# Key sums on TensorE for the first twelve head pairs, weight rounding on ScalarE, and an order that knows the shared port

## The chip, the cores and the metric

The kernel runs on one core of one Trainium2 chip. The metric is the device time of one execution in microseconds (us); of the kernel before there are three timed runs, 1079.8, 1080.3 and 1081.45 us, with a median of 1080.3 us. Five engines work side by side: PE (TensorE, whose weight loads are a row of their own, PEld), DVE (VectorE), ACT (ScalarE), POOL (GpSimd) and SP, which here only issues DMAs.

## The reference

An attention with random features feeds a gated two-layer network.

```python
# attention: batch 8, 8 heads, 576 rows, head dimension 64, 128 features
phi(x) = exp(x @ omega.T - |x|^2/2 - max over features) / sqrt(128)   # x scaled by 64**-0.25
q_p, k_p = phi(q), phi(k)
kv  = sum over rows s of k_p[s, m] * v[s, d]
z   = sum over rows s of k_p[s, m]
num = q_p @ kv
den = (q_p @ z) + 1e-6
x   = num / den                      # 4608 tokens x 512
# network: 512 -> 2048 -> 512
h = x @ w_in
out = (h * sigmoid(h)) @ w_out
```

The weights `w_in` and `w_out` arrive as 64-bit floats, everything else in 32 bits.

## The kernel before, in words

**Attention.** The 64 heads are worked in 32 pairs, called windows in the code and pairs here, numbered 0 to 31. The 2 x 576 rows of a pair lie as nine chunks of 128 rows; the fifth chunk holds the last 64 rows of the first head and the first 64 of the second. For keys (k) and queries (q) alike: PE projects eight chunks into two PSUM banks (`project`, L304) and the mixed chunk into a third (`project_mid`, L311); ACT squares the rows and DVE sums the squares (L292, L296); DVE takes the maxima (L318, L320), makes the shift from them (`shift`, L324 and L325), and ACT takes the exponential, for pairs 0 to 7 straight from PSUM (L340), from pair 8 on in one piece over all nine chunks after DVE has lowered them into SBUF (L345, L348, L354).

Then comes the part that the change touches. POOL adds up the key exponentials of each head over its chunks (`sums`, L360, L362, L365: 1,152 columns become 2 x 128). PE multiplies the 256 sums by a matrix of ones, so that every partition holds both key sums (`zsum`, L369). ACT copies them from PSUM to SBUF in three blocks, for the first head, the mixed chunk and the second head (`zcopy`, L377, L378). DVE multiplies each of the nine query chunks with its block and accumulates along the row (`denom`, L405, with an accumulator read behind each), and takes the reciprocals (L410). POOL scales the query exponentials with them, three chunks at a time (`normal`, L415). PE transposes the nine chunks (`turn`, L421), ACT copies them out (L425), and PE multiplies them by the pair's key-value matrix (`numer`, L438; `kv`, L385, makes that matrix). ACT and DVE split the product into a high and a low part, the network's input x (L457, L461).

**Weights.** 32 blocks of 128 x 512 are turned from 64-bit to 32-bit floats by one ACT instruction (L488) and three DVE instructions each (`word`, L500, L502, L506), and then split: POOL rounds the high part (`weight_high`, L516) and subtracts it for the low one (`weight_low`, L520). Later POOL makes eight sets of sums of `w_out` blocks (L536 to L539) and splits those as well (L543, L547).

**Network.** Each product is three passes of 128 x 512 on PE (L567: high by high, high by low, low by high). The first tile of 512 tokens uses the weights as they come; the later tiles are worked in pairs with seven products in place of eight, read their split weights back from DRAM, and need ACT (L600, L609) and DVE (L605, L613) for activations, differences and low parts.

**Order.** Nothing orders itself at run time: each engine works its queue in order. The queues come from a list scheduler in the file (`Plan`). Each unit of work has an engine, a planned duration, a key (when it is wanted), the units it needs, and the ring buffers and PSUM banks it takes and frees; `run` repeatedly takes the unit that can start first. The pool of banks `att` has two banks. Pools `acc` (four) and `h` (two) are open to attention only before the network needs them, and `acc` again between the first tile's end and the first paired tile.

## Time and profile before

| | |
|---|---|
| timed runs, median | 1080.3 us |
| profiled execution | 1083.05 us |
| its span | 1081.3 us |
| instructions | 16865 |
| granted PE clock, mean | 0.968 |

| engine | busy us | share of the span |
|---|---|---|
| PE | 1010.0 | 93% |
| DVE | 755.3 | 70% |
| ACT | 633.2 | 59% |
| POOL | 323.7 | 30% |

The span is what the profile covers; the time of the same execution is 1.75 us longer. Shares over the whole span hide that the program has stages: PE is busy 5 to 7 tenths of the first 81 us, nearly all of the time from about 330 us on, and in between by turns. So the profile is read by stretches.

### The profile page before, as it was taken

The page shows a single profiled execution, that of the slowest core. Times are in us where ns is not written, and L with a number is a line of the kernel's source. Part 1 is how long each engine was busy: PE and PEld are TensorE (multiplying, and loading weights), DVE is VectorE, ACT ScalarE, POOL GpSimd, SP SyncE. Part 2 cuts the span into 40 slices and gives each one's busy share as a digit, 9 for nine tenths or more (in the row PEclk, how much of TensorE's full clock was granted, in tenths as well). Part 3 has the DMA queues.
Part 4 walks back from the last instruction along what each step waited for, and adds up shares of the span by engine and source line. Part 5 has one row for each costly group of instructions (what it writes and reads, how often), then busy time and mean ns, then how long its engine had stood idle before and what let it go on. Part 6 is the DMA issues. An engine that isn't in the chain of part 4 may idle for free.

```text
span 1081.3 us, 16865 instructions
## 1 busy us (share of the span) xinstructions
PE 1010.0 (93%) x5708; PEld 797.7 (74%) x5708; DVE 755.3 (70%) x1761; ACT 633.2 (59%) x1155; POOL 323.7 (30%) x390
## 2 busy tenths in 40 slices
PE   5667999898879999999999999999999999999998
PEld 4445767576657877777777777777777788888886
DVE  6897797978855789866677888667667642323565
ACT  4667768566546666666666667666666433333343
POOL 2665465586872122222122221222222100000000
PEclk7687999999989999999999999999999999999999
DMA  8686686788767666767766567666644586665454
GB/s 292 222 264 211 205 270 236 253 297 283 245 209 258 200 197 194 233 201 223 236 219 199 181 211 247 200 221 230 195 147 140 178 293 212 213 200 189 160 183 149
DMA packets 96325, 235.01 MB, mean 217 GB/s; under 512 B 17264, under 2 KB 33776, under 8 KB 96240
## 3 DMA queue, kind: packets, MB, share of 16 engines
q1 hardware_dynamic: 96096, 233.87, 65.8%
q8 instruction: 46, 0.75, 0.3%
q14 instruction: 39, 0.32, 0.1%
q10 hardware_dynamic: 144, 0.07, 0.0%
HBM read 197.20 MB, written 36.70 MB: 216 GB/s over the span
## 4 chain that ended last, share of the span: by engine, by line
PE 73%; DVE 18%; ACT 4%; issue 3%; POOL 1%; DMA 1%; SPq 0%; DVEq 0%; ACTq 0%; POOLq 0%
PE ps_h L567 30%; PE ps_acc L567 28%; DVE prod L405 5%; PE ps_att L304 4%; PE ps_att L385 3%; PE ps_att L421 2%; PE ps_att L438 2%; DVE g L502 1%; DVE mxk L320 1%; DVE mxq L320 1%; DVE g L500 1%; PE ps_att L311 1%; DVE g L506 1%; DVE nbk L324 1%; PE ps_att L369 1%
## 5 line engine op out<-in xcount | busy, mean ns | idle before, releaser
L567 PE MATMUL ps_h<-x,w 128*128 128x512 f32 x1728 | 452.0, 404 | 0.6 <-POOL w L520 0.6
L567 PE MATMUL ps_acc<-ts,wo 128*128 128x512 f32 x1536 | 384.0, 395 | 0.2 <-DVE nbq L324 0.2
L567 PEld LDWEIGHTS ps_h<-x,w 128*128 128x128 f32 x1728 | 319.0, 191 | 71.1 <-POOL w L520 1.5
L567 PEld LDWEIGHTS ps_acc<-ts,wo 128*128 128x128 f32 x1536 | 284.4, 188 | 60.1 <-POOL wo L520 0.7
L613 DVE TENSOR_TENSOR ts<-g,ts 128x512 fp32r<-128x512 f32 x224 | 159.2, 723 | 128.4 <-ACT ts L609 127.7
L609 ACT CAST ts<-g 128x512 fp32r<-128x512 f32 x224 | 138.7, 622 | 116.0 <-PE ps_acc L567 81.6
L415 POOL TENSOR_TENSOR hq<-hq,rd 128x384 f32<-128x384 f32 x96 | 90.5, 967 | 309.7 <-DVE rd L410 290.8
L600 ACT ACTIVATE g<-ps_h 128x512 f32<-128x512 f32 x128 | 76.6, 598 | 148.5 <-PE ps_h L567 147.1
L405 DVE CUSTOM_DVE_ANT_0 prod<-hq,zb 128x128 f32<-128x128 f32 x288 | 97.3, 338 | 50.7 <-ACT zb L378 31.3
L605 DVE TENSOR_TENSOR g<-g,g 128x1024 f32<-128x1024 f32 x64 | 79.8, 1255 | 32.2 <-ACT g L600 32.2
L360 POOL TENSOR_TENSOR t<-hk 128x256 f32<-128x256 f32 x64 | 49.2, 789 | 151.6 <-ACT hk L354 132.2
L354 ACT ACT_TABLE_LOAD x46 | 59.0, 1283 | 28.4 <-DVE hk L345 14.2
L600 ACT ACT_TABLE_LOAD x44 | 56.5, 1283 | 0.8
L292 ACT ACTIVATE nat<-nat 128x576 f32<-128x576 f32 x64 | 43.5, 686 | 15.6 <-DMA nat<-qn 9.4
L320 DVE TENSOR_REDUCE mxq<-ps_att 128x4 f32<-128x512 f32 x53 | 34.2, 684 | 24.0 <-PE ps_att L304 24.0
L425 ACT COPY en<-ps_att 128x384 f32<-128x384 f32 x76 | 34.8, 478 | 22.4 <-PE ps_att L421 21.8
L385 PE MATMUL ps_att<-hk,v 128*64 128x128 f32 x580 | 41.4, 293 | 4.1 <-issue 2.3
L304 PE MATMUL ps_att<-oms,rawq 64*128 64x128 f32 x424 | 36.7, 294 | 8.8 <-ACT zb L378 5.7
L304 PEld LDWEIGHTS ps_att<-oms,rawq 64*128 64x128 f32 x424 | 30.4, 195 | 19.0 <-ACT zb L378 6.9
L385 PEld LDWEIGHTS ps_att<-hk,v 128*64 128x64 f32 x580 | 34.0, 146 | 14.1 <-issue 10.6
L421 PE MATMUL ps_att<-ident,hq 128*128 128x128 f32 x228 | 36.7, 283 | 8.1 <-DVE hk L348 3.9
L421 PEld LDWEIGHTS ps_att<-ident,hq 128*128 128x128 f32 x228 | 27.6, 144 | 17.1 <-issue 6.7
(139 smaller groups left out, 1185.5 us busy)
## 6 DMA issues: line engine op xcount, KB each, us to landing
w<-w_d SPq DMA_DIRECT2D x128, 512.0 KB, 3.7
wo<-w_d SPq DMA_DIRECT2D x112, 512.0 KB, 4.4
rawk<-kT SPq DMA_DIRECT2D x32, 352.0 KB, 4.4
rawq<-qT SPq DMA_DIRECT2D x32, 352.0 KB, 4.3
...
```

The lines of the kernel that those rows point to most:

```text
L304: nc.tensor.matmul(ps[:, i * M : (i + 1) * M], raw[r, o : o + P], oms[r], start=True, stop=True)
L320: nc.vector.tensor_reduce(m[:, 5 * j : 5 * j + 4], ps.rearrange("p (c m) -> p c m", m=M), AX.X, ALU.max)
L354: nc.scalar.activation(h, h, AF.Exp)
L385: nc.tensor.matmul(ps[j * D : (j + 1) * D, :M], vt[:, c + j], e[:, c], start=i == 0, stop=i == 4)
L405: nc.vector.tensor_tensor_reduce(out=prod, in0=e[:, c], in1=zb[:, j], scale=1.0, scalar=GUARD, op0=ALU.mult, op1=ALU.add, accum_out=den[:, ...
L415: nc.gpsimd.tensor_tensor(e[:, c], e[:, c], rd[:, c].unsqueeze(2).broadcast_to([P, 3, M]), ALU.mult)
L421: nc.tensor.transpose(ps[:, i * P : (i + 1) * P], T["h", n, "q"][:, 3 * g + i], ident)
L567: nc.tensor.matmul(ps, w(a), x[:, b], start=first and n == 0, stop=last and n == 2, **more)
L600: nc.scalar.activation(T["g", p, q, u][:, f % 2], T["ph", t, f], AF.Silu)
L605: nc.vector.tensor_tensor(out, a, b, ALU.subtract)
L609: nc.scalar.copy(g[:, 0], T["g", p, SOURCE[j], i // 2][:, i % 2])
L613: nc.vector.tensor_tensor(g[:, 1], T["g", p, SOURCE[j], i // 2][:, i % 2], g[:, 0].bitcast(F32), ALU.subtract)
```

## The change

- `FEW = 12`. For pairs 0 to 11, `sums`, `zsum` and `zcopy` are gone. `zsum_all` takes their place: twenty matmuls of 128 columns on PE, whose moving operand is the key exponentials themselves and whose stationary operand is ones, or, for the mixed chunk, `half`, ones in one head's partitions and zeros in the other's. They leave the three blocks side by side in one PSUM bank. Five go into all 128 partitions for each head; for the mixed block five go into partitions 0 to 63 and then five into 64 to 127.
- For those pairs `denom` reads the blocks from PSUM, and the bank is free only after the ninth chunk. The scaling is one DVE instruction over 1,152 columns (`normal_all`) in place of three on POOL. Pairs 12 to 31 are as before.
- The rounding of the high parts, 32 blocks and 16 of the sums, goes from POOL to ACT (`nc.scalar.copy`).
- The scheduler gets a time `port` that the marked units share: POOL's, and those of DVE with two SBUF operands, may not overlap in its plan. Most planned durations and DMA times are lowered, by about an eighth; `den` goes from 2.3 to 3.1 and `wlo` from 1.05 to 1.3.

```diff
+FEW = 12
@@ Plan
-    def add(self, name, eng, dur, key, fn, after=(), order=(), alloc=(), free=(), banks=0, table=None, lat=0.0):
+    def add(self, name, eng, dur, key, fn, after=(), order=(), alloc=(), free=(), banks=0, table=None, lat=0.0, port=False):
...
-                    t = max(t, free_at[e])
+                    t = max(t, free_at[e], port if u["port"] else 0.0)
...
+            if u["port"]:
+                port = t + dur
@@ attention_mlp
+    half = const.tile([P, 2, P], F32, tag="half", name="half")
+    nc.vector.memset(half, 0.0)
+    for j in range(2):
+        nc.vector.memset(half[j * D : (j + 1) * D, j], 1.0)
...
+    def zsum_all(n, ps):
+        e = T["h", n, "k"]
+        for b, (j, cols, rows) in enumerate(((0, P, 0), (0, D, 0), (1, D, D), (1, P, 0))):
+            at = (0, 1, 1, 2)[b] * M
+            for i in range(5):
+                nc.tensor.matmul(
+                    ps[rows : rows + cols, at : at + M], half[:, j, :cols] if i == 4 else ones[:, :cols],
+                    e[:, MID if i == 4 else 5 * j + i], start=i == 0, stop=i == 4,
+                )
+        T["zb", n] = ps[:, : 3 * M].rearrange("p (j m) -> p j m", m=M)
+
+    def normal_all(n):
+        e, rd = T["h", n, "q"], T["rd", n]
+        nc.vector.tensor_tensor(e, e, rd.unsqueeze(2).broadcast_to([P, NC, M]), ALU.mult)
...
-        nc.gpsimd.tensor_copy(parts_of(i)[0], T["w", i])
+        nc.scalar.copy(parts_of(i)[0], T["w", i])
...
-        nc.gpsimd.tensor_copy(o[:, 0], T["whole", i][:, b])
+        nc.scalar.copy(o[:, 0], T["whole", i][:, b])
@@ the units of a pair
+        few = n < FEW
+        if few:
+            add(zn, "PE", 1.8, at(n, 6, 26), lambda ps, n=n: zsum_all(n, ps), after=e["k"] + e["q"], banks=1, free=[("h", n, "k")],
+                order=[("z", n - 1)] if n else [])
+        else:
+            add(("sums", n), "POOL", 3.2, at(n, 6, 25), lambda n=n: sums(n), after=e["k"], port=True,
...
-        add(("den", n), "DVE", 2.3, at(n, 8, 34.2), lambda n=n: denom(n), after=e["q"] + [("zc", n)],
-            order=[("den", n - 1)] if n else [], alloc=[("den", ("den", n)), ("rd", ("rd", n))], free=[("zb", n)])
+        add(("den", n), "DVE", 3.1, at(n, 8, 34.2), lambda n=n: denom(n), after=e["q"] + [zn if few else ("zc", n)],
+            order=[("den", n - 1)] if n else [], alloc=[("den", ("den", n)), ("rd", ("rd", n))],
+            free=[bk(zn) if few else ("zb", n)], port=not few)
+        if few:
+            add(("norm", n, 0), "DVE", 1.25, at(n, 9, 37), lambda n=n: normal_all(n), after=[("den", n)],
+                free=[("rd", n)], port=True)
@@ the weights
-        add(("wh",) + i, "POOL", 0.9, key - 1, lambda: weight_high(i), after=[("wd",) + i + (2,)], alloc=list(more))
-        add(("wlo",) + i, "POOL", 1.05, key, lambda: weight_low(i), after=[("wh",) + i])
+        add(("wh",) + i, "ACT", 0.55, key - 1, lambda: weight_high(i), after=[("wd",) + i + (2,)], alloc=list(more))
+        add(("wlo",) + i, "POOL", 1.3, key, lambda: weight_low(i), after=[("wh",) + i], port=True)
```

The order moves with it. Line numbers are those of each file: L304, L311, L369, L385, L393, L405, L461, L500, L502, L506, L520 and L567 of the kernel before are L311, L318, L390, L407, L415, L427, L483, L522, L524, L528, L542 and L589 of the changed one.

PE from the products of pair 4 (`en,kw`) to the projection of pair 6 (`oms,rawk`), before:

```order
L438 MATMUL ps_att<-en,kw 64x64 x2
L567 MATMUL ps_h<-x_918,w_978 128x512 x3
L567 MATMUL ps_acc<-ts,wo 128x512 x9
L369 MATMUL ps_att<-es,ones 128x256
L567 MATMUL ps_acc<-ts,wo 128x512 x3
L393 MATMUL ps_att<-ident,kt 128x128
L567 MATMUL ps_h<-x_386,w_1123 128x512 x3
L567 MATMUL ps_h<-x_575,w_1123 128x512 x3
L567 MATMUL ps_h<-x_753,w_1123 128x512 x3
L304 MATMUL ps_att<-oms,rawk 128x128 x8
```

The same place in the changed kernel, from the last fifteen of the twenty matmuls on:

```order
L379 MATMUL ps_att<-hk,ones 64x128 x4
L379 MATMUL ps_att<-hk,half 64x128
L379 MATMUL ps_att<-hk,ones 64x128 x4
L379 MATMUL ps_att<-hk,half 64x128
L379 MATMUL ps_att<-hk,ones 128x128 x4
L379 MATMUL ps_att<-hk,half 128x128
L589 MATMUL ps_acc<-ts,wo 128x512 x12
L415 MATMUL ps_att<-ident,kt 128x128
L589 MATMUL ps_h<-x_372,w_1186 128x512 x3
L589 MATMUL ps_h<-x_573,w_1186 128x512 x3
L311 MATMUL ps_att<-oms,rawk 128x128 x8
```

One matmul of 256 columns became twenty of 128, and between them and the next projection, which takes both banks of `att`, stand 18 network matmuls where 12 stood.

DVE ahead of the denominators of pair 4, which begin four rows behind this piece (one more of those rows is a weight block's L506); L500, L502 and L506 are the three instructions of a weight block. Before:

```order
L506 SCALAR_TENSOR_TENSOR g_748<-g_584,g_748 128x512
L500 TENSOR_SCALAR g_849<-g_742 128x512
L500 TENSOR_SCALAR g_890<-g_745 128x512
L502 SCALAR_TENSOR_TENSOR g_890<-g_890 128x512
L506 SCALAR_TENSOR_TENSOR g_890<-g_745,g_890 128x512
L318 TENSOR_REDUCE mxq<-ps_h 128x1
L461 TENSOR_TENSOR x_918<-ps_att,x_918 128x512
L461 TENSOR_TENSOR xr<-ps_att,xr 128x64
L324 TENSOR_TENSOR nbq<-mxq,sqq 128x1
L325 SCALAR_TENSOR_TENSOR nbq<-nbq,sqq 128x1
L502 SCALAR_TENSOR_TENSOR g_849<-g_848,g_849 128x512
```

And in the changed kernel, down to the first row of those denominators:

```order
L528 SCALAR_TENSOR_TENSOR g_489<-g_400,g_489 128x512
L303 TENSOR_REDUCE sqk<-nat 128x9
L522 TENSOR_SCALAR g_489<-g_617 128x512
L522 TENSOR_SCALAR g_715<-g_622 128x512
L524 SCALAR_TENSOR_TENSOR g_715<-g_715 128x512
L528 SCALAR_TENSOR_TENSOR g_715<-g_622,g_715 128x512
L303 TENSOR_REDUCE sqq<-nat 128x9
L483 TENSOR_TENSOR x_956<-ps_acc,x_956 128x512
L483 TENSOR_TENSOR xr<-ps_acc,xr 128x64
L427 ISA prod,den<-hq,ps_acc 128x128
```

Counted from the program's start, DVE has finished 11 weight blocks at this point before and 8 now; the denominators read `ps_acc`, a PSUM bank, in place of `zb`.

POOL's first work, before:

```order
L360 TENSOR_TENSOR t<-hk 128x256 x2
L362 TENSOR_TENSOR es<-t 128x256
L365 TENSOR_TENSOR es<-es,hk 64x128 x2
L415 TENSOR_TENSOR hq<-hq,rd 128x384 x3
L516 CAST w_309<-g_253 128x512
L520 TENSOR_TENSOR w_309<-g_253,w_309 128x512
```

And in the changed kernel, where up to the sums of `w_out` blocks only low parts are left on it:

```order
L542 TENSOR_TENSOR w_436<-g_250,w_436 128x512
L542 TENSOR_TENSOR w_442<-g_277,w_442 128x512
L542 TENSOR_TENSOR wo<-g_274,wo 128x512
L542 TENSOR_TENSOR w_627<-g_483,w_627 128x512
L542 TENSOR_TENSOR wo<-g_274,wo 128x512
```

More of the change, by code (lines that the diff above doesn't have):

```diff
@@ L692, in attention_mlp @@
             for j in range(3):
-                add(("top", n, who, j), "DVE", 0.3 if j == 2 else 0.7,
+                add(("top", n, who, j), "DVE", 0.26 if j == 2 else 0.62,
                     at(n, 3 * i + 1 + 0.1 * j, o + 1.2 + (4.5 if j == 2 else 0.1 * j)),
@@ L707, in attention_mlp @@
                 if n < DIRECT:
-                    add(("exp", n, who, j), "ACT", 0.4 if j == 2 else 1.15,
+                    add(("exp", n, who, j), "ACT", 0.35 if j == 2 else 1.05,
                         at(n, 3 * i + 2 + 0.1 * j, o + 1.6 + (4.4 if j == 2 else 0.1 * j)),
@@ L711, in attention_mlp @@
                 else:
-                    add(("low", n, who, j), "DVE", 0.36 if j == 2 else 0.7,
+                    add(("low", n, who, j), "DVE", 0.3 if j == 2 else 0.62,
                         at(n, 0, o + 1.5 + (4.4 if j == 2 else 0.1 * j)),
@@ L715, in attention_mlp @@
             if n >= DIRECT:
-                add(("expall",) + w, "ACT", 1.2, at(n, 0, 24 + 0.1 * i), lambda n=n, who=who: expo_all(n, who),
+                add(("expall",) + w, "ACT", 1.1, at(n, 0, 24 + 0.1 * i), lambda n=n, who=who: expo_all(n, who),
                     after=[("low", n, who, j) for j in range(3)], table="exp")
@@ L723, in attention_mlp @@
             plan.freed_by[("nb", n, who)] = [("exp" if n < DIRECT else "low", n, who, j) for j in range(3)]
[L724 to L725 removed]
         zn = ("z", n)
[L727 to L729 removed]
+        few = n < FEW
[4 more added lines that the diff above has]
+            add(("sums", n), "POOL", 3.2, at(n, 6, 25), lambda n=n: sums(n), after=e["k"], port=True,
+                order=[("sums", n - 1)] if n > FEW else [],
+                alloc=[("t", ("t", n)), ("es", ("es", n))], free=[("h", n, "k"), ("t", n)])
+            add(zn, "PE", 0.45, at(n, 7, 32), lambda ps, n=n: zsum(n, ps), after=[("sums", n)], banks=1, free=[("es", n)])
+            add(("zc", n), "ACT", 1.1, at(n, 7.1, 33.2), lambda n=n: zcopy(n), after=[zn],
+                order=[("zc", n - 1)] if n > FEW else [], alloc=[("zb", ("zb", n))], free=[bk(zn)])
         merged = n > LEAD
@@ L798, in attention_mlp @@
         last = ("out", f)
-        add(("keep2", f), "SP", 0.8, key + 4, lambda f=f: keep_second(f), after=[("wlo", "out", f)], lat=2.1,
+        add(("keep2", f), "SP", 0.8, key + 4, lambda f=f: keep_second(f), after=[("wlo", "out", f)], lat=1.75,
             free=[("wo", 0, f)])
@@ L837, in first @@
         if t == 0:
-            add(("silu", 0, f), "ACT", 1.22, key, lambda: silu(f), after=[done], alloc=[("ts", ("ts", 0, f))], table="silu")
-            add(("gl", f), "DVE", 0.7, key + 1.3, lambda: g_low(f), after=[("silu", 0, f)], free=[("ph", 0, f)])
+            add(("silu", 0, f), "ACT", 1.1, key, lambda: silu(f), after=[done], alloc=[("ts", ("ts", 0, f))], table="silu")
+            add(("gl", f), "DVE", 0.62, key + 1.3, lambda: g_low(f), after=[("silu", 0, f)], free=[("ph", 0, f)])
             return
@@ L846, in first @@
             guard = [[("wd", "out", FIRST[-1], 2)], [("co", NH - 1, 1)]][t - 1]
-        add(("silu", t, f), "ACT", 0.62, key, lambda: silu_kept(t, f), after=[done], table="silu", order=guard,
+        add(("silu", t, f), "ACT", 0.55, key, lambda: silu_kept(t, f), after=[done], table="silu", order=guard,
             alloc=[] if f % 2 else [(f"g{QUARTERS[p % 2][q]}", ("g", p, q, f % NH // 2))], free=[("ph", t, f)])
@@ L886, in differences @@
         for d in range(4):
-            add(("dif", p, d, u), "DVE", 1.2, key[d], lambda d=d: subtract(p, d, u), after=needs[d],
+            add(("dif", p, d, u), "DVE", 1.2, key[d], lambda d=d: subtract(p, d, u), port=True, after=needs[d],
                 free={2: [("g", p, 3, u)], 3: [("g", p, 0, u)]}.get(d, []))
@@ L899, in times @@
             add(("w2", p, j, u), "SP", 0.42, mm_time(pos - 14 * AHEAD_W2), lambda: get_second(p, j, u), after=w,
-                order=seconds[-1:] or [("wh", "out", FIRST[-1])], alloc=[("wo", ("w2", p, j, u))], lat=2.1)
+                order=seconds[-1:] or [("wh", "out", FIRST[-1])], alloc=[("wo", ("w2", p, j, u))], lat=1.75)
             seconds.append(("w2", p, j, u))
@@ L903, in times @@
         src = [("g", p, SOURCE[j], u)] if j in (P6, P3, P7, P4) else []
-        add(("hi", p, j, i), "ACT", 0.62, key - 4, lambda: part_high(p, j, i), after=ready(p, j, i), order=highs[-1:],
+        add(("hi", p, j, i), "ACT", 0.54, key - 4, lambda: part_high(p, j, i), after=ready(p, j, i), order=highs[-1:],
             alloc=[("ts", ("ts", p, j, i))], free=src)
-        add(("lo", p, j, i), "DVE", 0.69, key - 3, lambda: part_low(p, j, i), after=[("hi", p, j, i)], order=lows[-1:],
+        add(("lo", p, j, i), "DVE", 0.66, key - 3, lambda: part_low(p, j, i), port=True, after=[("hi", p, j, i)], order=lows[-1:],
             free=src)
@@ L955, in times @@
             add(("store", p, what), "SP", 0.42, key + 2, lambda: c_store(p, what, PAIRS[p][t], d),
-                after=[(unit, p, m) for m in range(2)], lat=2.1, free=[("c", p, what)])
+                after=[(unit, p, m) for m in range(2)], lat=1.75, free=[("c", p, what)])
     for x, f in enumerate(FIRST):
```

72 lines of the change are left out of this document (34 added, 38 removed).

## The prediction

> **What bounds the kernel now.** I read the windows view first, cut where the network's stream starts (101 us), where PE first loses its density (190 us), where the attention falls behind the network no more (328 us), and where attention ends. Its columns are busy us with instruction counts for PE, PEld, DVE, ACT and POOL, then the granted PE clock.
>
> ```profile
> 0.00:101.00 101.00, 63.74 (x437) 47.30 (x438) 83.62 (x217) 62.33 (x183) 53.51 (x69) 0.75 0.74 251
> 101.00:190.00 89.00, 84.22 (x471) 65.39 (x469) 71.76 (x158) 66.52 (x138) 49.01 (x52) 1.00 0.70 232
> 190.00:328.00 138.00, 115.19 (x714) 87.28 (x716) 107.00 (x259) 80.25 (x135) 98.07 (x121) 0.94 0.76 259
> 328.00:856.00 528.00, 526.02 (x3120) 416.12 (x3116) 390.79 (x990) 343.53 (x568) 123.08 (x149) 1.00 0.64 205
> ```
>
> Four stages with different limits. Stage A (0 to 101): DVE is busy 83.6 of 101 us, PE 63.7 at a clock of 0.75; DVE leads. Stage B (101 to 190): PE is busy 84.2 of 89; PE bounds, and 4.8 us are left. Stage C (190 to 328): PE 115.2 of 138, so 22.8 us are left; DVE 107 and POOL 98 are both high. Stage D: PE 526 of 528, nothing to gain there, and since pairs 12 to 31 keep their work, nothing much to lose.
>
> Then the chain of waits (start, length, what), of which these pieces show who leads in A and in C:
>
> ```profile
> 22.80 2.81 POOL hq L415 x3
> 30.94 2.00 POOL t L360 x2
> 98.45 6.99 PE ps_h L567 x24
> 105.44 2.72 PE ps_acc L567 x12
> 305.67 1.33 DVE prod L405
> ```
>
> In A, POOL's key sums and scaling stand on the chain. In C it is DVE's denominators, and one chunk takes 1.33 us there. The network's matmuls take 2.72 / 12 = 0.227 us each once they flow; the first 24 of them took 6.99 in place of 5.44. The timeline adds PE's own waits in A, at the transposes of pairs 2 to 4:
>
> ```profile
> 61.87 1.69 PE L421 MATMUL ps_acc<-ident,hq 128*128 128x128 f32 x6 [3.31 <-POOL hq L415]
> 77.66 0.55 PE L421 MATMUL ps_acc<-ident,hq 128*128 128x128 f32 x3 [1.63 <-POOL hq L415]
> 95.97 2.48 PE L421 MATMUL ps_acc<-ident,hq 128*128 128x128 f32 x9 [3.03 <-POOL hq L415]
> ```
>
> **Part 1, key sums on PE.** The price of a full-width 128-column matmul in 32 bits is read from two starts in stage D, and that of a half-width one, whose neighbours run in the other half of the array, from the key-value product:
>
> ```profile
> 344.68 0.38 PE L311 MATMUL ps_att<-oms,rawk 128*128 128x128 f32 x2
> 344.89 0.49 PE L421 MATMUL ps_att<-ident,hq 128*128 128x128 f32 x3
> 327.27 1.31 PE L385 MATMUL ps_att<-hk,v 128*64 128x128 f32 x20
> 328.41 1.14 PE L438 MATMUL ps_att<-en,kw 128*64 128x512 f32 x8
> 85.94 2.40 PE L385 MATMUL ps_att<-hk,v 128*64 128x128 f32 x20 [2.34 <-issue]
> ```
>
> One matmul (two records) takes 344.89 - 344.68 = 0.21 us. The ten of L385, alternating between the halves, take 328.41 - 327.27 = 1.14, or 0.114 each. The new five-and-five half-width ones don't alternate, so I price all twenty at 0.213: 4.27 us. The old matmul has 256 columns: 0.43. Net +3.84 us per pair; the lower bound, half of them at 0.114, is 10 x 0.213 + 10 x 0.114 - 0.43 = 2.84. At half clock (L385 takes 2.40 there, twice as long) it is 8.5.
>
> Where it lies: pairs 5, 6 and 7 fall in B, 3 x 3.84 = 11.5 us against 4.8 idle. I let half of that idle take it up: **B +9** (bounds +4, the cheap price with all the idle used, and +12). Pairs 8 to 11 fall in C, 15.4 us against 22.8 idle: no cost there while another engine leads. What hides it is DVE; without that cover it costs the 15.4. In A the old way to the denominators was POOL's sums, the matmul and ACT's copies:
>
> ```profile
> L360 POOL TENSOR_TENSOR t<-hk 128x256 f32<-128x256 f32 x12 | 9.4, 800 | 12.3 <-ACT hk L340 12.3
> L362 POOL TENSOR_TENSOR es<-t 128x256 f32<-128x256 f32 x6 | 5.1, 848 | 0.5
> L365 POOL TENSOR_TENSOR es<-es,hk 64x128 f32<-64x128 f32 x10 | 6.4, 644 | 0.7
> L415 POOL TENSOR_TENSOR hq<-hq,rd 128x384 f32<-128x384 f32 x15 | 12.4, 854 | 19.8 <-DVE rd L410 19.8
> L378 ACT COPY zb<-ps_acc 128x128 f32<-128x128 f32 x6 | 1.6, 264 | 0.1
> ```
>
> 2 x 0.80 + 0.85 + 2 x 0.64 = 3.7 on POOL, 0.43 / 0.75 = 0.6 on PE, 4 x 0.264 = 1.1 on ACT: 5.4 us. The new one is 4.27 / 0.75 = 5.7. I take nothing for it (bounds -1 and +3 a pair, full and half clock).
>
> [...]
>
> **Part 2, POOL emptied, DVE relieved.** DVE instructions with two SBUF operands are stretched where POOL works. First their rows in A, then in C, then D's row and whole-run minima, medians and maxima as the undisturbed price:
>
> ```profile
> L405 DVE CUSTOM_DVE_ANT_0 prod<-hq,zb 128x128 f32<-128x128 f32 x45 | 15.9, 353 | 4.0 <-ACT zb L378 1.5
> L506 DVE SCALAR_TENSOR_TENSOR g<-g,g 128x512 uint32<-128x512 uint32 x11 | 9.5, 860 | 0.2
> L500 DVE TENSOR_SCALAR g<-g 128x512 uint32<-128x512 uint32 x12 | 7.3, 621 | 0.0
> L502 DVE SCALAR_TENSOR_TENSOR g<-g 128x512 uint32<-128x512 uint32 x6 | 6.3, 1043 | 0.6
> L405 DVE CUSTOM_DVE_ANT_0 prod<-hq,zb 128x128 f32<-128x128 f32 x45 | 21.9, 486 | 2.3
> L324 DVE TENSOR_TENSOR nbk<-mxk,sqk 128x8 f32<-128x8 f32 (+1 forms) x12 | 6.0, 502 | 0.4
> L324 DVE TENSOR_TENSOR nbq<-mxq,sqq 128x8 f32<-128x8 f32 (+1 forms) x12 | 5.8, 480 | 0.4
> L405 DVE CUSTOM_DVE_ANT_0 prod<-hq,zb 128x128 f32<-128x128 f32 x171 | 50.0, 292 | 43.2 <-ACT zb L378 29.8 <-ACT hq L354 4.3 <-ACT kw L398 0.5
> L506 DVE SCALAR_TENSOR_TENSOR g<-g,g x32: 631/693/1660, 22.5 to 224.8; 128x512 uint32<-128x512 uint32 x32
> L500 DVE TENSOR_SCALAR g<-g x32: 410/421/1511, 18.1 to 218.2; 128x512 uint32<-128x512 uint32 x32
> L324 DVE TENSOR_TENSOR nbq<-mxq,sqq x60: 151/169/1291, 11.7 to 831.7; 128x8 f32<-128x8 f32 x28, 128x1 f32<-128x1 f32 x28, 128x9 f32<-128x9 f32 x4
> L605 DVE TENSOR_TENSOR g<-g,g 128x1024 f32<-128x1024 f32 x64 | 79.8, 1255 | 32.2 <-ACT g L600 32.2
> ```
>
> In A: 45 x 0.061 = 2.7 for the denominators, 11 x 0.167 + 12 x 0.200 + 6 x 0.35 = 6.3 for the weights (L502 priced like L506). POOL loses 12.4 + 9.4 + 5.1 + 6.4 = 33.3 and ten roundings of some 0.7, 40 of its 53.5 us. The denominators no longer read two SBUF operands, so I take their 2.7 whole and three quarters of the 6.3: -7.4. Added: five scalings of 1,152 columns at 1.255 x 1.1 = 1.4 (L605 has 1,024), +6.9. The order puts three weight blocks behind pair 4, at 0.42 + 0.69 + 0.69 = 1.8 each: -5.4, worked off in B where DVE has 17 us free. Scaling takes 1.4 in place of 3 x 0.85 = 2.55 and starts at once behind the reciprocals: -1.1 for each of the three quoted waits, -3.5. Sum -9.4; I take **A -9**, at most -15 if the small shift instructions, which I have not counted, are relieved too.
>
> In C: the denominators lose 45 x 0.194 = 8.7, of which pairs 8 to 11 are four fifths, -7.0; of the shifts' 6.0 + 5.8 - 24 x 0.17 = 7.7 a third, as POOL keeps two thirds of its work (sums of `w_out` and pairs from 12 on), -2.6; four scalings +5.5. That is -4. Transposes there also wait for scalings that queue behind those sums, by the view of waits:
>
> ```profile
> PEld ps_att L421 <- POOL c L543: 2.8, 1, 2.8
> PEld ps_att L421 <- POOL g L537: 2.7, 1, 2.7
> ```
>
> I take half of these 5.5, so **C -7**, just what PE allows: 22.8 - 15.4 = 7.4 (bounds -7, and +8 if half of the 15.4 shows).
>
> The denominators' second operand now comes from PSUM. No row has that form; bounds are 0 (a two-operand 512-column instruction from PSUM, L636, next) and the 0.06 by which L345 at 128 columns exceeds L405's 0.292, some 5 us over nine pairs of A and C. I take 0, since L636's 683 lies under the median 691 of its SBUF counterpart L613.
>
> ```profile
> L636 DVE TENSOR_TENSOR c<-ps_acc,c 128x512 f32<-128x512 f32 x48 | 31.7, 683 | 2.1 <-PE ps_acc L567 2.1
> L613 DVE TENSOR_TENSOR ts<-g,ts x224: 639/691/1317, 231.4 to 1073.4; 128x512 fp32r<-128x512 f32 x112
> L345 DVE TENSOR_SCALAR hk<-ps_att,nbk 128x128 f32<-128x128 f32 x23 | 8.1, 351 | 0.8
> ```
>
> [...]
>
> **Part 3, rounding on ACT.** ACT has a cast of this shape:
>
> ```profile
> L609 ACT CAST ts<-g 128x512 fp32r<-128x512 f32 x224 | 138.7, 622 | 116.0 <-PE ps_acc L567 81.6 <-DVE ts L613 33.1 <-ACT ts L609 0.8
> ```
>
> Forty-eight at 0.62 are 30 us, less twelve times the 1.1 of the copies: +17 us up to 340 us, on an engine with 62 + 67 + 80 = 209 of the first 328 busy. What hides it is ACT's idle time; uncovered, an ACT cast that waits for DVE's last weight word holds the exponentials queued behind it. I take 0; bounds 0 and +5.
>
> **Sum.** -9 + 9 - 7 = -7 on the profiled 1083.05 us (its span 1081.3): 1076. The median lies 2.75 lower, so **1073 us**; with its own range 1062 to 1080.
>
> **The rivals.** *Cheap matmuls* (faster): the half-width groups overlap, B +4, and A reaches -15, C -7: -18, 1062. For: L385's halves do overlap; against: five in a row share a half. *Nothing net*: DVE's relief in A stays off the chain, because its 17 idle us are waits on other engines: A -2, B +9, C -7: 1080. *Cold array* (slower): in A the twenty stay at half clock, 8.5 in place of 5.4 us on the way to each of four pairs' denominators, +12, less the scaling's 3; in B no idle takes any, +12; C is left at 0: +21, 1101. It decides once A's clock stays at or below 0.75 with the sums in it. *The bank* (slower): the PSUM bank of the sums is held through 4.27 + 9 x 0.37 = 7.6 us in place of 0.43 + 1.1, and the next projection needs both banks of its pool. Eighteen network matmuls of 0.227 (4.1 us) cover 3.4 of denominators, if DVE starts them at once; if it comes 2.5 us late in each of pairs 5 to 11, PE loses 17: 1090. Decides once DVE is over 0.7 us late.
>
> **How the numbers follow.** Forecast 0.46, cheap matmuls 0.14, nothing net 0.08, cold array 0.18, the bank 0.14. About 0.2% is what the timing tells from no change: faster 0.60, same 0.08, slower 0.32. The range runs from 1056 (below the cheap case, by the uncounted shifts) to 1095, which holds the bank and leaves most of the cold case out.
>
> **What would show it.** The changed profile should have twenty matmuls taking 4.2 to 4.4 us at full clock; the denominators at 0.29 to 0.30 in all stages; POOL's busy time down by about 100 us; the start of the dense network stream 8 to 10 us before 98; and PE without idle at all up to the fourth pair behind it. A stream that starts later than 98, projections waiting for DVE's `prod`, or a PE clock under 0.75 in A would make the prediction wrong.

## The result, and the profile after

The changed kernel takes 1087.8 us (median of four runs, 1086.0 to 1089.0), the kernel before, on the same chip, 1080.7 (1079.8 to 1081.45). The ratio is 1.0065 with a 95% interval of 1.0047 to 1.0082: 7.1 us slower, where 1073 us, a gain of some 7, was forecast. The profiled execution took 1088.49 us, its span is 1086.7.

The windows view of the changed kernel, cut as before (busy us with counts for PE, PEld, DVE, ACT, POOL; granted PE clock; DMA share; GB/s):

```profile
0.00:101.00 101.00, 78.46 (x631) 63.82 (x632) 72.35 (x223) 63.69 (x174) 12.12 (x14) 0.85 0.70 232
101.00:190.00 89.00, 86.69 (x508) 69.49 (x507) 68.18 (x144) 72.10 (x138) 24.54 (x18) 1.00 0.76 243
190.00:328.00 138.00, 129.16 (x916) 102.90 (x915) 96.99 (x273) 86.12 (x139) 58.03 (x60) 0.98 0.81 268
328.00:856.00 528.00, 523.82 (x3112) 413.17 (x3111) 389.66 (x999) 346.68 (x573) 116.61 (x155) 1.00 0.63 203
```

By this view the relief came. DVE has 11 us less in the first stage and 10 less in the third, POOL falls from 53.5 to 12.1 and from 98 to 58, and the PE clock of the first stage rises from 0.75 to 0.85. But PE is the busier by 14.7, 2.5 and 14.0 us, and no stage is shorter by more than 1.3 us, as the following reckoning has it.

How much each stage gained is read from the products of pairs 4, 6 and 13, which end roughly at the stages' borders. Their starts in the timeline, first of the kernel before, then of the changed one (start us, length us, what):

```profile
116.99 1.14 PE L438 MATMUL ps_att<-en,kw 128*64 128x512 f32 x8
185.41 1.14 PE L438 MATMUL ps_att<-en,kw 128*64 128x512 f32 x8
362.78 1.14 PE L438 MATMUL ps_att<-en,kw 128*64 128x512 f32 x8
```

```profile
114.68 1.14 PE L460 MATMUL ps_att<-en,kw 128*64 128x512 f32 x8
193.52 1.14 PE L460 MATMUL ps_att<-en,kw 128*64 128x512 f32 x8
364.09 1.14 PE L460 MATMUL ps_att<-en,kw 128*64 128x512 f32 x8
```

The two orders have not issued the same amount of network work by then: 81, 288 and 696 matmuls of the network stand ahead of these products before, 75, 309 and 693 after, at 0.227 us each. The difference in time less that of the work is -2.3 + 1.4 = **-0.9 us** at pair 4, 8.1 - 4.8 = **+3.3** at pair 6, 1.3 + 0.7 = **+2.0** at pair 13, and at the end of the span **+5.4**. By stages: A -0.9 (forecast -9), B +4.2 (+9), C -1.3 (-7), D +3.4 (0). I call this the lag at a pair. Two executions of one order can be compared by it; between different orders, as here, it is loose, because an order can put the network ahead of the attention and lose nothing by it. The kernel with the new order alone (1070.2 us below) shows how loose:

```profile
142.97 1.14 PE L460 MATMUL ps_att<-en,kw 128*64 128x512 f32 x8
```

At pair 4 it has 159 network matmuls behind it and lags the kernel before by 26.0 - 17.7 = 8.3 us, and yet its span is 14.8 us shorter. So the split by stages is a sketch; the prices below are read from whole times, and between kernels of one order.

The chain of waits of the changed kernel says why A and C gave so little. Here are its pieces of the key sums (L379), then one of them with what follows it, first and last of nine (start, length, what):

```profile
16.78 5.02 PE ps_acc L379 x40
36.40 4.58 PE ps_acc L379 x40
53.69 4.39 PE ps_att L379 x40
71.14 5.16 PE ps_acc L379 x40
96.73 6.89 PE ps_h L589 x24
```

```profile
118.38 4.64 PE ps_att L379 x40
158.78 4.66 PE ps_att L379 x40
```

```profile
196.93 4.39 PE ps_att L379 x40
201.34 0.29 DVE prod L427
...
203.98 0.29 DVE prod L427
230.49 4.39 PE ps_att L379 x40
266.16 4.39 PE ps_att L379 x40
286.15 4.39 PE ps_att L379 x40
301.71 4.57 PE ps_acc L379 x40
```

In eleven of the twelve pairs the sums stand on the chain, 19.2 us of it up to the dense stream, 9.3 in B and 22.1 in C. DVE's nine denominators need PE's last matmul, and in eight of the eleven they come right behind it on the chain; behind the pieces at 118.38 and 301.71 comes PE's own next work. The network's dense stream starts at 96.73 in place of 98.45, less than 2 us earlier. The view of waits for the first 328 us says the same of DVE:

```profile
DVE prod L427 <- PE ps_att L379: 22.2, 7, 5.6
DVE prod L427 <- PE ps_acc L379: 9.1, 3, 3.9
```

31.3 us of DVE's idle time are waits for these sums; all its idle time ahead of the denominators was 7.5 us in the kernel before (its row stands with the port's runs below). DVE has less to do, and waits for the engine that now makes its input. The groups of DVE in A and in C (busy us, mean ns, idle before):

```profile
L427 DVE CUSTOM_DVE_ANT_0 prod<-hq,ps_acc 128x128 f32<-128x128 f32 x36 | 10.3, 287 | 11.7 <-PE ps_acc L379 6.6 <-PE ps_h L415 3.5
L387 DVE TENSOR_TENSOR hq<-hq,rd 128x1152 f32<-128x1152 f32 x5 | 6.8, 1353 | 0.1
```

```profile
L427 DVE CUSTOM_DVE_ANT_0 prod<-hq,ps_att 128x128 f32<-128x128 f32 x36 | 10.3, 287 | 16.6 <-PE ps_att L379 15.4
L387 DVE TENSOR_TENSOR hq<-hq,rd 128x1152 f32<-128x1152 f32 x5 | 8.4, 1685 | 0.1
```

The denominators take 287 ns in both stages, where they took 353 and 486. The scaling takes 1.35 and 1.69 us, against a forecast of 1.4.

### The profile page after: what moved, and what is told of

Its sections match the earlier page's. It is cut to its first block, busy times and chain, and to the rows that moved or that the text cites. A ratio compares the mean times of both kernels' runs of the same rounds, so it can differ in the third digit from the quotient of the medians.

```text
span 1086.7 us, 17554 instructions
## 1 busy us (share of the span) xinstructions
PE 1044.4 (96%) x6164; PEld 835.3 (77%) x6164; DVE 730.9 (67%) x1776; ACT 651.6 (60%) x1159; POOL 211.3 (19%) x246
## 4 chain that ended last, share of the span: by engine, by line
PE 81%; DVE 11%; ACT 3%; DMA 2%; issue 1%; POOL 0%; SPq 0%; DVEq 0%; ACTq 0%; POOLq 0%
PE ps_h L589 33%; PE ps_acc L589 29%; PE ps_att L311 4%; DVE prod L427 3%; PE ps_att L379 3%; PE ps_att L443 3%; PE ps_att L407 2%; PE ps_att L460 2%; PE ps_acc L379 2%; DMA nat<-qn 1%; DVE hq L387 1%; PE ps_att L318 1%; PE ps_att L391 1%; DVE mxk L327 1%; DVE ts L635 1%
## 5 line engine op out<-in xcount | busy, mean ns | idle before, releaser
L589 PE MATMUL ps_h<-x,w 128*128 128x512 f32 x1728 | 452.0, 402 | 0.2 <-POOL w L542 0.2
L589 PE MATMUL ps_acc<-ts,wo 128*128 128x512 f32 x1536 | 384.6, 395 | 0.2 <-ACT hq L347 0.2
L589 PEld LDWEIGHTS ps_h<-x,w 128*128 128x128 f32 x1728 | 316.1, 190 | 69.0 <-POOL w L542 1.2
L589 PEld LDWEIGHTS ps_acc<-ts,wo 128*128 128x128 f32 x1536 | 284.7, 188 | 61.4 <-ACT hq L347 0.6
L635 DVE TENSOR_TENSOR ts<-g,ts 128x512 fp32r<-128x512 f32 x224 | 155.4, 709 | 112.8 <-ACT ts L631 112.3
L437 POOL TENSOR_TENSOR hq<-hq,rd 128x384 f32<-128x384 f32 x60 | 55.9, 959 | 286.5 <-DVE rd L432 272.0
L427 DVE CUSTOM_DVE_ANT_0 prod<-hq,zb 128x128 f32<-128x128 f32 x180 | 52.6, 292 | 45.4 <-ACT zb L400 35.9
L367 POOL TENSOR_TENSOR t<-hk 128x256 f32<-128x256 f32 x40 | 30.4, 781 | 132.4 <-ACT hk L361 132.4
L542 POOL TENSOR_TENSOR w<-g,w 128x512 fp32r<-128x512 f32 x16 | 23.4, 1468 | 143.4 <-ACT w L538 122.5
L311 PEld LDWEIGHTS ps_att<-oms,rawq 64*128 64x128 f32 x408 | 27.7, 190 | 11.9 <-ACT en L447 6.1
L311 PE MATMUL ps_att<-oms,rawq 64*128 64x128 f32 x408 | 33.4, 289 | 2.9 <-ACT en L447 2.7
L407 PEld LDWEIGHTS ps_att<-hk,v 128*64 128x64 f32 x520 | 28.4, 139 | 9.6 <-issue 8.6
```

The costliest lines, as they stand in the source:

```text
L311: nc.tensor.matmul(ps[:, i * M : (i + 1) * M], raw[r, o : o + P], oms[r], start=True, stop=True)
L407: nc.tensor.matmul(ps[j * D : (j + 1) * D, :M], vt[:, c + j], e[:, c], start=i == 0, stop=i == 4)
L427: nc.vector.tensor_tensor_reduce(out=prod, in0=e[:, c], in1=zb[:, j], scale=1.0, scalar=GUARD, op0=ALU.mult, op1=ALU.add, accum_out=den[:, ...
L437: nc.gpsimd.tensor_tensor(e[:, c], e[:, c], rd[:, c].unsqueeze(2).broadcast_to([P, 3, M]), ALU.mult)
L589: nc.tensor.matmul(ps, w(a), x[:, b], start=first and n == 0, stop=last and n == 2, **more)
L635: nc.vector.tensor_tensor(g[:, 1], T["g", p, SOURCE[j], i // 2][:, i % 2], g[:, 0].bitcast(F32), ALU.subtract)
```

## The experiments

Each kernel was timed in five rounds beside the kernel before, whose medians were 1080.5 to 1081.3 us. So times of different rows can be compared to within some 1 us. The edits are to the changed kernel unless another is named; six more kernels are given in the text.

| edit | us (range) | ratio to before, 95% |
|---|---|---|
| old sums and scaling, all pairs | 1067.1 (1066.3 to 1068.2) | 0.9866 to 0.9891 |
| the same, rounding on POOL: the order alone | 1070.2 (1067.4 to 1072.7) | 0.989 to 0.992 |
| rounding on POOL | 1080.0 (1077.4 to 1082.7) | 0.9984 to 1.0004 |
| half-width matmuls by turns | 1079.4 (1076.6 to 1082.1) | 0.9981 to 1.0002 |
| new sums and scaling for pairs 0 to 3 | 1076.7 (1076.3 to 1077.3) | 0.9942 to 0.9969 |
| old sums, scaling on DVE | 1078.3 (1076.9 to 1080.4) | 0.9958 to 0.9982 |
| new sums, scaling on POOL | 1086.2 (1083.2 to 1087.7) | 1.0029 to 1.0065 |
| old sums and scaling, no port in the plan | 1091.4 (1089.3 to 1093.5) | 1.0076 to 1.0105 |
| kernel before with the port alone | 1077.2 (1075.3 to 1078.2) | 0.9955 to 0.9979 |
| four fifths of the sums left out | 1058.7 (1058.4 to 1061.8) | 0.9789 to 0.982 |
| the same for pairs 0 to 4 | 1075.8 (1073.9 to 1077.1) | 0.9941 to 0.9969 |
| sums planned at 4.3 us | 1083.5 (1079.6 to 1085.0) | 1.0013 to 1.0033 |

### Undoing the parts: sums, rounding, order

My first theory, P, was that PE's sums had taken the lead from DVE. Rivals were O, that the new planned numbers make a worse order, and R, that the rounding on ACT holds the exponentials up.

```diff
-FEW = 12
+FEW = 0
```

> The changed kernel with FEW = 0: all 32 pairs add their key sums and scale on POOL as before; rounding on ACT and the new planned numbers stay. Theory P (PE took the lead: with the key sums in it PE is the last to finish in every stretch up to 328 us, so DVE's relief is not used and each early pair pays some 4 us of PE time): without them PE loses 46 us of work and DVE gets the shared port back, so 1076 to 1082 us, faster than the changed kernel by 6 to 12, with PE busy under 75 of the first 101 us. Rival O (the new planned numbers give a worse order): 1086 or more, since the numbers stay. Rival R (exponentials held behind ACT's rounding): 1085 or more, since the rounding stays on ACT.

```diff
-FEW = 12
+FEW = 0
-        nc.scalar.copy(parts_of(i)[0], T["w", i])
+        nc.gpsimd.tensor_copy(parts_of(i)[0], T["w", i])
-        nc.scalar.copy(o[:, 0], T["whole", i][:, b])
+        nc.gpsimd.tensor_copy(o[:, 0], T["whole", i][:, b])
-        add(("wh",) + i, "ACT", 0.55, key - 1, lambda: weight_high(i), after=[("wd",) + i + (2,)], alloc=list(more))
+        add(("wh",) + i, "POOL", 0.65, key - 1, lambda: weight_high(i), port=True, after=[("wd",) + i + (2,)], alloc=list(more))
...
```

The sixteen roundings of the sums (`ch`) are planned on POOL in the same way.

> Only the scheduler of the change: FEW = 0 and rounding on POOL (planned at 0.65 us, with the port), so every instruction is that of the kernel before and only the order differs. Theory P: the numbers matter little, 1078 to 1085 us, with at most 3 us lost behind 328 us, where the changed kernel lost 2.7. Rival O: 1088 or more. Rival R: 1080 or less, since no rounding is on ACT.

The third kernel has the second's rounding lines, and FEW stays at 12.

> The changed kernel with the rounding back on POOL (planned at 0.65 us, with the port); the key sums stay on PE. Theory P: PE leads all the same, 1086 to 1091 us. Rival R: 1080 or less, because the exponentials no longer wait behind casts. Rival O: 1086 to 1090 as well.

With the old sums the change is 1067.1 us, faster than both kernels by 13.4 and 20.7: the sums and the scaling together cost 20.7 us. With the old sums and the rounding on POOL it is 1070.2: O falls, the new order alone is worth 10.3. P had the sign and missed the size, 1076 to 1082 and 1078 to 1085, since it gave the order no gain. Its 1086 to 1091 for the third kernel missed too (1080.0): rounding on ACT gains 3.1 us without the new sums and costs 7.8 with them. That looked like R; a later run took it away again.

A fourth kernel asks for the price of PE's time. The ten half-width matmuls of the mixed block are issued by turns, so that neighbours write different halves of the partitions:

```diff
-        for b, (j, cols, rows) in enumerate(((0, P, 0), (0, D, 0), (1, D, D), (1, P, 0))):
+        whole, mixed = [(0, P, 0, 0)], [(0, D, 0, M), (1, D, D, M)]
+        for group in (whole, mixed, [(1, P, 0, 2 * M)]):
             for i in range(5):
+                for j, cols, rows, at in group:
...
```

> The changed kernel with the ten half-width matmuls of a pair's key sums issued alternately for the two halves of the array, in place of five and five. Theory P: a pair's sums take some 3.3 us at full clock in place of 4.3, and as PE leads up to 328 us about 1 us is saved for each of the twelve pairs: 1076 to 1081 us. Rivals O and R: PE's work is not what decides, so 1085 to 1088.

In its chain two of the sums read:

```profile
192.18 3.68 PE ps_att L380 x40
225.06 3.68 PE ps_att L380 x40
```

3.68 in place of 4.39: 0.71 us less for a pair, 8.5 for twelve. The time fell by 8.4. By these medians a microsecond of the sums costs a microsecond of the kernel; the ranges leave 2 to 3 us of play.

### Which half of it, and which part of the order

```diff
-FEW = 12
+FEW = 4
```

> The changed kernel with FEW = 4: only pairs 0 to 3 have their key sums on PE and are scaled on DVE. With FEW = 0 the time is 1067.1 us, with 12 it is 1087.8. Theory P2 (in the first stretch the sums stand on the chain of each pair, since DVE waits for them; so PE's idle time there hides nothing): 1073 to 1079 us. Rival A (the first stretch has idle PE enough and the loss comes from pairs 4 to 11 alone, as the prediction had it for the first stretch): 1065 to 1069.

The first four pairs alone cost 9.6 us over the old sums. This is as P2 had it, and it speaks against the step by which the first stage paid nothing.

```diff
-        few = n < FEW
+        few = False
         if few:
             add(zn, "PE", 1.8, at(n, 6, 26), lambda ps, n=n: zsum_all(n, ps), after=e["k"] + e["q"], banks=1, free=[("h", n, "k")],
...
+        few = n < FEW
         if few:
             add(("norm", n, 0), "DVE", 1.25, at(n, 9, 37), lambda n=n: normal_all(n), after=[("den", n)],
```

> The changed kernel with the key sums on POOL and ACT's copies for all pairs, but the scaling of pairs 0 to 11 on DVE in one instruction. Theory P2 (the loss is that of the key sums on PE): 1063 to 1069 us, about as with FEW = 0. Rival D (DVE cannot take the 1.35 us of scaling for each pair): 1075 to 1088.

1078.3, as rival D had it: scaling on DVE with the old sums costs 11 us. Its groups and waits over the first 328 us show where PE waits:

```profile
L427 DVE CUSTOM_DVE_ANT_0 prod<-hq,zb 128x128 f32<-128x128 f32 x117 | 50.9, 435 | 9.5 <-ACT hq L361 2.2 <-ACT zb L400 1.4
L387 DVE TENSOR_TENSOR hq<-hq,rd 128x1152 f32<-128x1152 f32 x12 | 18.0, 1499 | 0.3
```

```profile
PE ps_acc L443 <- DVE nbk L331: 14.8, 2, 8.6
PE ps_h L443 <- DVE g L522: 9.1, 1, 9.1
PE ps_att L443 <- DVE hq L387: 7.7, 2, 5.8
```

These transposes wait 31.6 us for DVE, 7.7 of them for the scaling by name; for the rest another DVE instruction is named. Then the other half, sums on PE with the scaling left in three instructions on POOL:

```diff
         plan.freed_by[("den", n)] = [("den", n)]
+        few = False
         if few:
             add(("norm", n, 0), "DVE", 1.25, at(n, 9, 37), lambda n=n: normal_all(n), after=[("den", n)],
```

> The changed kernel, but the scaling of pairs 0 to 11 is back in three instructions on POOL; their key sums stay on PE. The old sums with the old scaling took 1067.1 us, the old sums with scaling on DVE 1078.3, the changed kernel 1087.8. Theory A (both halves cost, and each about its own price: PE's sums stand on every pair's way in the first stage, scaling loads the engine that leads): 1075 to 1080. Theory B (nearly all of the loss is the scaling on DVE; PE's sums are hidden once DVE is free of it): 1066 to 1071. Theory C (nearly all of it is PE's sums): 1083 to 1088.

1086.2, as theory C had it: PE's sums alone cost 19.0 us. The two halves cost 11.1 and 19.0, and together 20.7, not 30. Where PE's sums are there, scaling on DVE adds only 1.7, less than these orders scatter (see below). It looks as if a delay of either kind on a pair's way covers the other; no run shows this by itself.

Now the order. One kernel takes the port out of the planner:

```diff
-FEW = 12
+FEW = 0
-                    t = max(t, free_at[e], port if u["port"] else 0.0)
+                    t = max(t, free_at[e])
```

> FEW = 0, rounding on ACT, and the scheduler without the shared port (the units' start no longer waits for it); planned durations as in the change. Theory S (the gain of the new order comes from the port): 1074 to 1082 us. Rival N (it comes from the new planned durations): 1064 to 1070.

The time is 1091.4: with the new durations the port is worth 24.3 us, far past what either theory expected. The denominators of the first 328 us, without the port in the plan, and with it (the kernel of 1067.1 us):

```profile
L427 DVE CUSTOM_DVE_ANT_0 prod<-hq,zb 128x128 f32<-128x128 f32 x117 | 47.9, 410 | 9.1 <-ACT zb L400 2.4 <-ACT hq L361 0.6
```

```profile
L427 DVE CUSTOM_DVE_ANT_0 prod<-hq,zb 128x128 f32<-128x128 f32 x126 | 41.9, 333 | 8.6 <-ACT zb L400 1.4 <-ACT hq L361 0.5
```

The same instruction, on the same operands in SBUF, takes 333 ns in place of 410; the two kernels differ in their order alone. In the kernel before, 90 of the 117 denominators of this stretch ran with no POOL instruction beside them and took 0.28 to 0.29 us; the 27 that ran beside one took 0.78 on average and up to 1.33 (the one at 305.67, beside a POOL instruction of 1.29 that began at 305.57). The plan that means to keep the two apart takes most of the excess over the undisturbed 292 ns away, 77 of 118 ns.

Does the port help by itself? The kernel before, with the port for the same units and nothing else:

```diff
-                    t = max(t, free_at[e])
+                    t = max(t, free_at[e], port if u["port"] else 0.0)
...
+            if u["port"]:
+                port = t + dur
...
-        add(("wlo",) + i, "POOL", 1.05, key, lambda: weight_low(i), after=[("wh",) + i])
+        add(("wlo",) + i, "POOL", 1.05, key, lambda: weight_low(i), after=[("wh",) + i], port=True)
...
```

The other units that the change marks get the same `port=True`, and POOL's rounding with them; all durations, the sums and the scaling are those of before.

> The kernel before with one thing of the change: the planner's reservation of the shared port, for the same operations as in the change. Planned durations, sums, scaling and rounding (on POOL) are those of before. Theory A (the reservation is worth its 24 us wherever it stands): 1055 to 1062. Theory B (it only repairs an order that the new durations spoiled, the one without it took 1091; with the old durations there is less to repair): 1070 to 1082.

1077.2 against 1080.5, as theory B had it: 3.3 us. The denominators of the first 328 us, in the kernel before and in this one:

```profile
L405 DVE CUSTOM_DVE_ANT_0 prod<-hq,zb 128x128 f32<-128x128 f32 x117 | 47.4, 405 | 7.5 <-ACT zb L378 1.5
```

```profile
L427 DVE CUSTOM_DVE_ANT_0 prod<-hq,zb 128x128 f32<-128x128 f32 x123 | 38.2, 311 | 12.9 <-ACT zb L400 6.6
```

They fall by 94 ns each, more than the 77 above, and yet the time falls by 3.3 us and not by 24.3. So shorter denominators are not what makes the 24.3; what does is not shown. The new durations and the rounding without the port lose 10, the port alone gains 3.3, all of it together gains 13.4. The gain of the order comes only with both of its parts. The kernel without the port was timed in one order.

Are these orders luck? Two kernels plan one copy at 0.44 in place of 0.42, which says nothing new and reorders most of each queue; the first has the old sums (1067.1), the second is the changed kernel (1087.8):

```diff
-            add(("en", n, g), "ACT", 0.42, at(n, 9.6 + 0.1 * g, 44.4 + 0.8 * g), lambda n=n, g=g: en_copy(n, g),
+            add(("en", n, g), "ACT", 0.44, at(n, 9.6 + 0.1 * g, 44.4 + 0.8 * g), lambda n=n, g=g: en_copy(n, g),
```

> The old sums and scaling with rounding on ACT and the new order (1067.1 us), but the planned duration of one copy (the transposed queries, on ACT) is 0.44 in place of 0.42, which says nothing new of the chip and yet reorders much of the program. Theory A (the order's gain comes from what it models): within 3 us of 1067. Theory B (these orders scatter by chance): off by 5 us or more.

> The changed kernel (1087.8 us) with the same nudge, 0.44 in place of 0.42 for the copy of the transposed queries. Theory A (its loss is in the work that was moved): within 3 us of 1088. Theory B (its loss is an unlucky order): off by 5 us or more, most likely to the fast side.

1069.5 (1066.6 to 1070.6) and 1088.3 (1086.4 to 1090.6): 2.4 and 0.5 us off. Other changes of planned durations, further down, move the time by up to 4.4 us, so differences of that size say little; the 20 us between these two kernels are far beyond that and are in the work.

### The price of the sums, in one order

The next two leave the queues as they are and leave work out: each block of a pair issues its last matmul alone (so the denominators of these pairs miss most keys).

```diff
+CUT = 12
...
-            for i in range(5):
+            for i in ((4,) if n < CUT else range(5)):
...
```

> The changed kernel, in the same order, with four fifths of the key sums left out: each of the four blocks of a pair issues one matmul in place of five, so the denominators of pairs 0 to 11 miss most of their keys. That takes 16 x 0.213 = 3.4 us of PE from each pair, 41 us in all. Theory P (the sums cost by the PE time they take, and about half of it finds idle time): 1064 to 1070. Theory D (with the sums gone, scaling on DVE leads, as in the run with scaling alone on DVE, 1078): 1075 to 1081. Theory M (the loss is not in the matmuls themselves but in an order planned for 1.8 us): 1084 to 1088.

> The same cut for pairs 0 to 4 alone, the pairs before the dense stream: 5 x 3.4 = 17 us of PE less in the first stage, nothing less later. Theory P with the loss on the way to the first denominators: 8 to 14 us back, 1074 to 1080. If PE's sums were covered in the first stage, as the prediction had it, and the loss lies in pairs 5 to 11: 1085 to 1088.

Chain pieces of the first (CUT = 12), and its products of pairs 4 and 13; then those of the second (CUT = 5):

```profile
209.82 1.02 PE ps_att L380 x8
244.08 1.02 PE ps_att L380 x8
```

```profile
100.49 1.14 PE L461 MATMUL ps_att<-en,kw 128*64 128x512 f32 x8
334.54 1.14 PE L461 MATMUL ps_att<-en,kw 128*64 128x512 f32 x8
```

```profile
99.16 1.14 PE L461 MATMUL ps_att<-en,kw 128*64 128x512 f32 x8
348.33 1.14 PE L461 MATMUL ps_att<-en,kw 128*64 128x512 f32 x8
```

The sums of a pair take 1.02 in place of 4.39: 3.37 us less, 40.4 for twelve pairs. The time falls by 29.1, to 1058.7, past theory P's 1064 to 1070: **by the medians, 72% of PE's time in the sums is paid**. Cut in the first five pairs alone (16.9 us) the time falls by 12.0, 71%, and pair 4's product comes 114.68 - 99.16 = 15.5 earlier (14.2 in the first, the same work up to there), so that most of it is on the way there. At pair 13 the two kernels are 364.09 - 334.54 = 29.6 and 364.09 - 348.33 = 15.8 us ahead of the changed one. The other seven pairs are the rest: 1075.8 - 1058.7 = 17.1 of 23.6, 72%. Neither stretch hides them. PE's idle time did not take them up in A either. The first 101 us of the first kernel:

```profile
0.00:101.00 101.00, 78.20 (x549) 59.56 (x551) 79.06 (x235) 75.96 (x197) 14.92 (x17) 0.85 0.77 257
```

PE is idle for 22.8 us with most of the sums left out and for 22.5 with all of them: they filled no gap, they pushed what follows them out.

At pair 4 the cut kernel is 100.49 - 116.99 + 1.4 = 15.1 us ahead of the kernel before, in the stage where I had forecast 9; how much of that is the relief comes below.

Last, the plan. It gives 1.8 us to sums that take 4.4. Two kernels give them their length, the second with rounding on POOL:

```diff
-            add(zn, "PE", 1.8, at(n, 6, 26), lambda ps, n=n: zsum_all(n, ps), after=e["k"] + e["q"], banks=1, free=[("h", n, "k")],
+            add(zn, "PE", 4.3, at(n, 6, 26), lambda ps, n=n: zsum_all(n, ps), after=e["k"] + e["q"], banks=1, free=[("h", n, "k")],
```

> The changed kernel with the sums planned at 4.3 us, what they take, in place of 1.8. Theory M (an order planned 2.5 us too short per pair makes the loss): 1068 to 1078. Theory P (the time of the matmuls makes it, whatever the plan says): 1084 to 1091.

> The changed kernel with rounding back on POOL (1080.0 us) and the sums planned at 4.3 us. Theory M: 1066 to 1075, faster than the kernel before. Theory P: 1077 to 1084.

The first gains 4.3 us and stays slower than before; the second is 1083.6 (1081.0 to 1085.5; ratio 1.0017 to 1.0039), 3.6 slower than with the wrong length. Theory M falls: an honest length is no cure. (P's 1084 to 1091 for the first missed by half a microsecond.) With it, rounding on ACT or POOL is the same, 1083.5 and 1083.6. So the 7.8 us that rounding on ACT seemed to cost beside the new sums belong to one pair of orders, not to the rounding.

### The stretch behind pair 13

The old durations for all paired tiles, with the old sums:

```diff
-FEW = 12
+FEW = 0
...
-        add(("hi", p, j, i), "ACT", 0.54, key - 4, lambda: part_high(p, j, i), after=ready(p, j, i), order=highs[-1:],
+        add(("hi", p, j, i), "ACT", 0.62, key - 4, lambda: part_high(p, j, i), after=ready(p, j, i), order=highs[-1:],
...
```

In the same way 0.55 becomes 0.62 for the activations, 0.63 and 0.66 become 0.69 on DVE, and 1.75 becomes 2.1 for these tiles' DMAs.

> FEW = 0, rounding on ACT, and the planned durations of the paired tiles (activations, high and low parts, sums of products, weight loads, stores) as before the change; those of attention and of the first tile as in the change. Behind 345 us PE waits four times for some 1 us at a pair's transposes in the changed kernel and with FEW = 0, and the kernel before does so once. Theory T (those waits come from the lowered durations of the paired tiles): 1062 to 1065 us. Rival: they come from those of attention, 1066 to 1069.

1071.5 (1071.1 to 1072.5; ratio 0.9894 to 0.992), 4.4 slower: theory T falls as a whole, and the rival's 1066 to 1069 misses as well, but the edit had moved the early orders too. So two more keep everything up to pair 16 alike and change the durations behind, with the old sums and in the changed kernel:

```diff
-        add(("hi", p, j, i), "ACT", 0.54, key - 4, lambda: part_high(p, j, i), after=ready(p, j, i), order=highs[-1:],
+        add(("hi", p, j, i), "ACT", 0.54 if p < 1 else 0.62, key - 4, lambda: part_high(p, j, i), after=ready(p, j, i), order=highs[-1:],
...
```

> The old sums and scaling with rounding on ACT and the new order (1067.1 us), but the paired tiles from the second couple on (from pair 20 or so) are planned with the durations of the kernel before: 2.1 in place of 1.75 for a DMA, 0.62 in place of 0.54 and 0.55 on ACT, 0.69 in place of 0.63 and 0.66 on DVE. Up to pair 16 each engine's order is the same. Theory T (the lower durations cost some 3 to 6 us behind 364 us): 1061.5 to 1064.5, below every version so far that computes all. Rival (what is lost there is a tail that any order pays): 1066.5 to 1068.

> The changed kernel (1087.8 us) with the same edit, also alike up to pair 16. Theory T: 1083 to 1085.5, 2.5 to 4.5 us back. Rival: 1087 to 1089.

1066.9 (1065.2 to 1068.0; ratio 0.9851 to 0.9889) and 1087.9 (1086.9 to 1090.9; ratio 1.0049 to 1.0084): no change, T falls for good. The second is useful in another way. Its queues are those of the changed kernel up to pair 16, and yet in its profile the product of pair 13 starts 3.2 us later than the 364.09 above (0.7 and 0.9 later at pairs 4 and 6; the profiled execution, 1090.9, is the slowest of its six):

```profile
367.32 1.14 PE L460 MATMUL ps_att<-en,kw 128*64 128x512 f32 x8
```

So a lag read from one execution is good to some 1 us up to pair 6 and 3 us at pair 13, and the +3.4 of stage D is hardly outside that. What the waits of PE behind 328 us show of it, before and after:

```profile
PE ps_att L421 <- DVE hk L348: 1.1, 1, 1.1
```

```profile
PE ps_att L443 <- DVE hk L355: 3.7, 4, 1.1
```

Four transposes wait about 1 us each for DVE where one did. The cause of this stays open.

## Why the prediction was wrong

**The step that failed is the price of the sums in stages A and C.** For A it read: "I take nothing for it (bounds -1 and +3 a pair, full and half clock)", since the old way took 5.4 us and the new one 5.7. With four fifths of the sums left out, in the same order, pair 4 comes 14.2 us earlier, 2.8 for each of five pairs; the gross price is paid. Against the old sums and scaling with the new durations and port (103.70, quoted next, with the same 75 network matmuls ahead of it, but another order), the new sums and scaling cost 114.68 - 103.70 = 11.0, or 2.2 a pair.

```profile
103.70 1.14 PE L460 MATMUL ps_att<-en,kw 128*64 128x512 f32 x8
```

Comparing lengths was the mistake. Nearly all of the old 5.4 us ran on POOL and ACT, while PE could project and transpose other pairs; the new 4.4 to 5.2 run on the engine that projections, transposes and products need as well. PE had 37 idle us in A, but leaving most of the sums out left its idle time where it was, 22.8 against 22.5, and the denominators wait for the sums. No run separates the two ways in which the sums cost: by holding up their own pair's denominators, and by keeping PE from other pairs.

For C it read: "no cost there while another engine leads. What hides it is DVE". DVE's denominators need the sums, so DVE could not hide them: in four of the five pairs whose sums lie in C, nine denominators follow right behind them on the chain. The 22.8 idle us of PE were real, but 72% of the sums' time is paid in pairs 5 to 11, B and C together. The prediction did state a price without that cover, 15.4 for four pairs; 72% of it is 11. (Its upper bound for C, +8, goes with the whole 15.4 and not with half of it: -7 + 7.7 is +0.7.)

**The relief (part 2) was right in its lengths and not in its worth.** POOL lost 112 us (forecast about 100), denominators take 287 ns (0.29 to 0.30), sums 4.39 at full clock (4.2 to 4.4). In A the kernel with most of the sums left out is 15.1 us ahead of the kernel before. But the old sums and scaling, with rounding on ACT and the new order, are already 11.9 ahead (103.70 - 116.99 + 1.4). That leaves some 3 us for the relief and the scaling, read across two orders; the 9 that were forecast are not shown to come from it.

**The order was not priced.** Only the three weight blocks that it puts behind pair 4 entered the sum. It is worth 10.3 us alone, and 13.4 with the rounding on ACT, by the port and the new durations together. This covers most of the loss: against the kernel with all of that and the old sums, the new sums and scaling cost 20.7 us, of which 7.1 are left to see. That the time came within 15 us of the forecast, and inside its range, is therefore luck: two misses of opposite sign, one on the price of the moved work and one on the order.

**Scaling on DVE** was counted among the gains ("-3.5" for three waits). Alone it costs 11.1 us, and PE's transposes then wait for DVE. Beside PE's sums it costs 1.7, which the orders' scatter does not tell from nothing.

**B** was forecast at +9 for three pairs, within +4 and +12; +4.2 was read, across two orders. In the changed kernel only pairs 5 and 6 have their sums in B (pair 7's begin at 196.93); the same working gives 2 x 3.84 - 2.4 = 5.3 for two. **Rounding on ACT** at 0 was right within the orders' scatter (-3.1, -0.1 and +7.8 in three pairs of orders). **D** at 0 was right but for up to 3.4 us, whose cause is open.

**The rivals.** *Cheap matmuls* falls: 4.39, not 3.3. *Cold array* falls at its own point: the clock in A is 0.85, not 0.75 or less. *The bank* falls: no pair's denominators begin more than 0.4 us behind its last matmul, where the rival needed 0.7, and projections waited 0.9 us in all for a bank held by the denominators; that its 1090 is the nearest number is luck. *Nothing net* was nearest by its A (-2 against -0.9), and also kept the gain in C that did not come.
